# First queries in two parts, one more tile turned by TensorE, and other steps for batch 1

## The chip, the cores and the metric

The kernel runs on one core of one Trainium2 chip. A core has five engines that run side by side, each through its own list of instructions in order: TensorE (PE; its weight loads are shown apart as PEld), VectorE (DVE), ScalarE (ACT), GpSimd (POOL) and SyncE (SP). They wait for each other by semaphores. SP, ACT and POOL also issue DMA transfers, each in a queue of its own; sixteen DMA engines serve all queues. The metric is the device time of one execution in microseconds (us); eight runs of the kernel before have a median of 226.18 us.

## The reference

```python
# attention: q, k, v are (4, 8, 768, 64); mem_k, mem_v are (4, 8, 8, 64)
for c in range(24):                      # chunks of 32 queries
    keys   = concat(mem_k, k[c*32-16 : c*32+40])    # cut at both ends of the sequence
    values = concat(mem_v, v[same rows])
    a = softmax(q[c*32 : c*32+32] @ keys.T / 8)
    x[c*32 : c*32+32] = a @ values
# then a feed-forward block on x, now (4, 768, 512)
xn = (x - mean(x)) / sqrt(var(x) + 1e-6) * g_ln
out = x + max(xn @ w_ch1, 0) @ w_ch2     # w_ch1 (512, 2048), w_ch2 (2048, 512)
```

## The kernel before

The work is cut into 24 tiles of 128 rows, six for each of the four batches. Three tiles make a unit, so there are eight units (0 to 7). For each tile attention runs first: `scores` multiplies keys and queries of two groups of 64 rows on PE, `soften` takes the exponential on ACT, `values` multiplies by the values on PE, and DVE divides by the sums, takes the mean and scales (`norm` writes `xn`). `turn_x` then transposes `xn` into `xT`, which the feed-forward part reads: `up` and `up_tile` multiply by w_ch1 (a relu on DVE or ACT takes the result out of PSUM), `down` multiplies by w_ch2, and `finish` adds and writes the output through SP.

Keys and queries come in blocks of 256 rows, three to a batch. A block is loaded with four rows of eight heads on a partition (`load_block`, through POOL, in 16-bit), put in another order (`mix`), transposed, and copied in windows to `KT` (`window`, `pieces`, `key_right`, `key_left`) and to `QR`. Each group of keys has 8 columns of mem keys at its end (`memT`, `mem_cols`), and each group of values 8 rows of mem values (`v_mem`). The first block of batch 0 is loaded in 32 bit through SP and ACT and cast by `mix_raw` instead, so that it is there early.

Where `turn_x` transposes is set by `XU = 2`: tiles of the first two units (0 to 5) are turned by four PE matmuls against the identity and a DVE copy out of PSUM, all later tiles by a DMA transpose issued on SP.

The order of the instructions on every engine is that of the program text; no scheduler moves anything. Three parts matter here. The start (L445 to L594) is written out by hand: it loads, sets constants, and interleaves the first three tiles' attention with pieces of unit 0's `up_tile`. `warm` issues matmuls of zeros. From there on, a table `plan` holds what is to be issued beside the feed-forward work: unit u has 28 steps, of which 0 to 15 are `up` groups and 16 to 27 `down` groups (four of 4 matmuls for each of three tiles), and `at(u, step, ...)` puts a call behind that step's group. `attend(i, s0, s1, u)` places the scores, values, `norm` and `turn_x` of tile i. PSUM has two slots `att` for attention and transposes and four slots `mm` for feed-forward groups and key transposes; each is taken in turn, so that a group waits until the copy or relu that empties its slot is done.

Names and lines for the steps: loads of keys, queries and mem keys at the start L446 to L453; the cast of mem keys (`memk16` from `memkf`) L529; the first tile's chain L527 to L557; scores of the second tile L558; mem values' rows `v_mem` L133; `turn_x` L343; `pace_x` L361, a small POOL copy that reads `xT` of a tile so that the loads queued behind it on POOL start no earlier; batch 1's steps in units 0 and 1 L655 to L677.

Of the kernel before, what the change touches and what calls it, by code (L numbers as in the profile page):

```python
# [15 lines left out]
def kernel(  # L16
# [12 lines left out]
    nc = tc.nc  # L29
# [9 lines left out]
    HD = 65  # L39
    XU = 2  # L40
    NEG = -30000.0
# [209 lines left out]

    def mix_raw(which, srcs, half, eng):

        o = pick(iv, ("b", 0, 0, which))
        for par in range(2):
            copy(eng, free(o, 512 * half + 64 * par, [[128, 4], [1, 64]]),
                 free(srcs[par], 256 * half, [[64, 4], [1, 64]]))

# [84 lines left out]
    def turn_x(b, t):  # L343
        i = NT * b + t
        dst = xT[(i // 3) % 2][:, :, 128 * (i % 3) : 128 * (i % 3) + 128]
        if i // 3 >= XU:
            nc.sync.dma_start_transpose(out=dst, in_=xn[i % 4])
            return
# [97 lines left out]
    nc.scalar.dma_start(out=grow, in_=dram(moe_g_ln, 0, [[512, 1], [1, 512]]))  # L446
    for which in range(2):
        for par, eng in ((0, nc.sync), (1, nc.scalar)):
            eng.dma_start(
                out=raws[which][par],  # L450
                in_=dram((k, q)[which], 4 * par * HS, [[512, 32], [HS, 4], [1, 512]]),
            )
    nc.scalar.dma_start(out=memkf, in_=dram(mem_k, 0, [[64, 128], [128 * 64, 2], [1, 64]]))  # L453

# [4 lines left out]

    load_mem_v(0, nc.sync)  # L460

    PAIR = 1.0 / 128 + 15.0 / 2**20
# [19 lines left out]
    make_identity(nc, identity)  # L482
    nc.gpsimd.memset(V[0][0:32, 0, :, :], 0.0)
    ones(0, 0, NG, pool)
    nc.vector.memset(zero, 0.0)
# [7 lines left out]
    nc.vector.tensor_tensor(out=band[:, 1:2], in0=band[:, 1:2], in1=cnt[:, 2:3], op=ALU.add)  # L493
    nc.vector.tensor_scalar(out=band, in0=band, scalar1=NEG, scalar2=None, op0=ALU.mult)

    load_block(0, 1, 0)
    load_v(0, 0)
# [35 lines left out]
    mem_keys()  # L533
    mix_raw(1, raws[1], 0, dve)
    mix_raw(1, raws[1], 1, act)
    transpose_block(0, 0, 1, Q0)
    window(0, 0, K0, 0, dve)
    memT()
    window(0, 0, K0, 1, act)
    mem_cols(0, dve)  # L540
    whole_q(0, 0, Q0)
    warm(1, 512, p[:, 1, :])
# [3 lines left out]
    soften(0, 0, 1)  # L546
    window(0, 0, K0, 2, dve)
    window(0, 0, K0, 3, act)
    total(cnt[:, 0:1], 16, 128)
    count_v(0, 0, 0)  # L550
    mix(0, 1, 0, dve)
    transpose_block(0, 1, 0, Q0)
    v_mem(0, 0, 2, dve)
    window(0, 1, Q0, 0, dve)
    key_right(0, 3, dve)
    values(0, 0)
    norm(0, 0)  # L557
    scores(0, 1)  # L558
    soften(0, 1, 0)
    soften(0, 1, 1)  # L560
    window(0, 1, Q0, 1, act)
    v_mem(0, 2, 4, dve)
# [37 lines left out]
    def attend(i, s0, s1, u):  # L600

        b, t = divmod(i, NT)
        at(u, s0, scores, b, t)
        at(u, s0, soften, b, t, 0)
        at(u, s0 + 1, soften, b, t, 1)
        at(u, s1, values, b, t)
        at(u, s1 + 1, norm, b, t)
        at(u, s1 + (3 if i // 3 < XU else 2), turn_x, b, t)
        at(u, s1 + 2, stats, b, t)
        if i < 6:  # L610
            at(1, i % 3, root, b, t)
        else:
            at(i // 3 - 1, (20, 22, 23)[i % 3], root, b, t)
# [43 lines left out]
    at(0, 22, mix, 1, 0, 0, dve)  # L657
    at(0, 27, mix, 1, 0, 1, dve)
    at(0, 27, v_mem, 1, 0, 4, dve)
    at(1, 0, turn_keys, 1, 0)  # L660
    at(1, 1, more_keys, 1, 0)
    at(1, 1, turn_queries, 1, 0)
    at(1, 2, mix, 1, 1, 0, dve)
    at(1, 4, mix, 1, 1, 1, dve)
    attend(6, 4, 8, 1)
    at(1, 6, turn_keys, 1, 1)
    at(1, 7, more_keys, 1, 1)
    at(1, 10, turn_queries, 1, 1)
# [87 lines left out]
```

## Time and profile before

| | |
|---|---|
| median of 8 runs | 226.18 us (225.65 to 230.3) |
| the profiled execution's own time | 226.02 us |
| its span, first to last instruction | 224.2 us |
| PE busy | 211.3 us (94%), 1941 matmuls |
| PE weight loads | 130.5 us (58%) |
| DVE busy | 133.1 us (59%) |
| ACT busy | 103.2 us (46%) |
| POOL busy | 100.2 us (45%) |
| DMA | 27.85 MB in 72737 packets, mean 124 GB/s |

Busy time is a share of the span; on PE it is the engine in work, not at its peak. The profile's pages give lines of kernel.py as L and a number; a copy or matmul made by a helper has the helper's line (L104 is every copy on DVE, L102 on ACT, L218 every transpose of a key or query block, L378 the up groups, L389 the up groups of single tiles, L404 the down groups). A chain of waits is followed back from the last instruction: each row is what the next one waited for. The granted clock is what the throttle allows of TensorE's clock.

### The profile page before, as it was taken

To read this page: it belongs to the slowest core of one execution; us is meant where nothing else is said; L and a number is where in the kernel's file an instruction comes from. 1 tells how busy PE (TensorE), PEld (TensorE's weight loads), DVE (VectorE), ACT (ScalarE), POOL (GpSimd) and SP (SyncE) were. 2 spreads that over 40 slices of the span, in tenths; PEclk is the share of its full clock that TensorE was granted. 3 is DMA by queue.
4 is the path that set the end of the run, shared out by engine and by line. 5 is a ranking of instruction groups with operands and counts; after the bars stand their busy time and mean duration, and the time that the engine had idled before them with its cause. 6 is when DMAs were issued, how large, how long until landed. Compare 5 with 4: busy or idle time off the path is not lost.

```text
span 224.2 us, 4942 instructions
## 1 busy us (share of the span) xinstructions
PE 211.3 (94%) x1941; PEld 130.5 (58%) x1941; DVE 133.1 (59%) x330; ACT 103.2 (46%) x215; POOL 100.2 (45%) x172
## 2 busy tenths in 40 slices
PE   7569999997999889999999999999999999999994
PEld 2357986555664457545664566446654566456553
DVE  4585586687869638745585668725845367234221
ACT  4452558535783146641692067524761365103200
POOL 8936744899898479320933793400021011100000
PEclk9999999999999999999999999999999999999998
DMA  5999999699999999978897699485112203211012
GB/s 183 182 193 195 198 193 206 109 84 233 177 80 148 188 169 141 161 157 197 109 178 86 100 160 150 90 196 131 21 30 70 96 5 45 70 49 45 3 47 94
DMA packets 72737, 27.85 MB, mean 124 GB/s; under 512 B 60785, under 2 KB 68721, under 8 KB 72714
## 3 DMA queue, kind: packets, MB, share of 16 engines
q0 software_dynamic: 45728, 14.61, 63.6%
q1 hardware_dynamic: 26424, 12.34, 24.5%
q10 hardware_dynamic: 562, 0.59, 0.9%
q8 instruction: 15, 0.25, 0.5%
q14 instruction: 8, 0.07, 0.1%
HBM read 30.28 MB, written 6.29 MB: 163 GB/s over the span
## 4 chain that ended last, share of the span: by engine, by line
PE 80%; DVE 7%; DMA 6%; ACT 3%; issue 1%; ACTq 1%; DVEq 0%; SPq 0%
PE mm L378 33%; PE mm L404 30%; PE att L283 5%; DMA xT<-xn 4%; PE mm L389 4%; PE att L304 4%; DMA memkf<-in_mem_k_dram 2%; PE mm L218 2%; PE mm L426 2%; DVE xs L312 1%; ACT AT L293 1%; DVE KT L104 1%; DVE xn L324 1%; DVE V L104 1%; DVE iv L104 1%
## 5 line engine op out<-in xcount | busy, mean ns | idle before, releaser
L404 PE MATMUL mm<-w2c,rT 128*128 128x512 f16 x368 | 82.8, 379 | 0.0
L378 PE MATMUL mm<-xT,w1c 128*128 128x384 f16 x448 | 78.6, 327 | 2.8 <-DMA xT<-xn 1.6
L378 PEld LDWEIGHTS <-w1c 128*128 128x128 f16 x448 | 49.0, 114 | 25.2 <-DVE osb L413 2.1
L404 PEld LDWEIGHTS <-rT 128*128 128x128 f16 x368 | 34.9, 98 | 39.7
L370 ACT ACTIVATE rT<-mm 128x384 f16<-128x384 f32 (+1 forms) x63 | 31.4, 503 | 41.2 <-PE mm L378 23.1
L372 DVE TENSOR_SCALAR rT<-mm 128x384 f16<-128x384 f32 (+1 forms) x61 | 34.3, 568 | 26.3 <-PE mm L378 23.0
L293 ACT ACTIVATE AT<-att,band 104x512 f16<-104x512 f32 x48 | 31.3, 685 | 30.5 <-PE att L283 30.5
L128 POOL DMA_DIRECT2D V<-in_v_dram x48 | 38.3, 804 | 5.0 <-DMA w1c<-in_moe_w_ch_dram 3.4
L413 DVE SCALAR_TENSOR_TENSOR osb<-mm,rstd,xs 128x512 f32<-128x512 f32 x23 | 17.3, 751 | 34.0 <-PE mm L404 25.0
L335 POOL TENSOR_SCALAR veps<-sq 128x1 f32<-128x1 f32 x24 | 7.7, 319 | 59.8 <-ACT junk L329 46.1
L329 ACT ACTIVATE junk<-xs,nmean 128x512 f16<-128x512 f32 x24 | 17.4, 723 | 14.9 <-DVE nmean L318 13.6
L324 DVE SCALAR_TENSOR_TENSOR xn<-xs,nmean,gb 128x512 f16<-128x512 f32 x24 | 17.9, 748 | 0.5
L312 DVE SCALAR_TENSOR_TENSOR xs<-att,rec 128x512 f32<-128x512 f32 x24 | 16.6, 691 | 0.8
L283 PE MATMUL att<-QR,KT 64*104 64x64 f16 x384 | 16.1, 235 | 0.3 <-ACT QR L102 0.2
L339 POOL TENSOR_TENSOR rstd<-veps,mhalf 128x1 f32<-128x1 f32 x24 | 15.2, 634 | 2.0
L283 PEld LDWEIGHTS <-KT 64*104 64x104 f16 x384 | 12.8, 134 | 4.2 <-issue 2.8
L120 POOL DMA_DIRECT2D st<-in_q_dram x22 | 12.6, 588 | 3.7 <-DMA w2c<-in_moe_w_ch_dram 1.7
L389 PE MATMUL mm<-xT,w1c 128*128 128x128 f16 x192 | 13.8, 235 | 0.5 <-DVE xT L357 0.5
L120 POOL DMA_DIRECT2D st<-in_k_dram x22 | 13.1, 613 | 2.3 <-DMA w1c<-in_moe_w_ch_dram 1.8
L389 PEld LDWEIGHTS <-w1c 128*128 128x128 f16 x192 | 12.7, 119 | 1.1 <-issue 1.0
L304 PEld LDWEIGHTS <-AT 104*64 104x64 f16 x384 | 8.4, 114 | 7.5 <-issue 4.6
L311 DVE RECIPROCAL rec<-att 128x8 f32<-128x8 f32 x24 | 4.9, 205 | 12.7 <-PE att L304 12.5
(73 smaller groups left out, 142.6 us busy)
## 6 DMA issues: line engine op xcount, KB each, us to landing
out_dram<-osb SPq DMA_DIRECT2D x23, 256.0 KB, 2.3
V<-in_v_dram POOLq DMA_DIRECT2D x40, 96.0 KB, 5.6
st<-in_k_dram POOLq DMA_DIRECT2D x22, 128.0 KB, 5.6
st<-in_q_dram POOLq DMA_DIRECT2D x22, 128.0 KB, 6.3
w1c<-in_moe_w_ch_dram POOLq DMA_DIRECT2D x4, 512.0 KB, 9.6
w2c<-in_moe_w_ch_dram POOLq DMA_DIRECT2D x4, 512.0 KB, 8.7
V<-in_v_dram POOLq DMA_DIRECT2D x8, 80.0 KB, 4.8
xT<-xn SPq DMA_TRANSPOSE x18, 2.4
```

What stands on the lines that cost most here:

```text
L120: nc.gpsimd.dma_start(out=s[:, 512 * par : 512 * par + 512], in_=dram((k, q)[which], (b * H + 4 * par) * HS + blk * 256 * D, [[512, 32], [ ...
L128: nc.gpsimd.dma_start(out=V[b % 2][lo:hi, g, :, 0:64], in_=dram(v, b * H * HS + (64 * g - 16 + lo) * D, [[64, hi - lo], [HS, H], [1, 64]]),)
L283: nc.tensor.matmul(out=p[0:W, par, (4 * gg + j) * 64 : (4 * gg + j) * 64 + 64], lhsT=KT[b % 2][rows, 2 * t + gg, j, :], rhs=free(QR[b % 2] ...
L293: nc.scalar.activation(out=free(AT[t % 3], 32 * c, [[64, 16], [1, 32]]), in_=free(p, 4 * c, [[64, 16], [1, 4], [8, 8]], W), func=ACTF.Exp, ...
L312: nc.vector.scalar_tensor_tensor(out=x.rearrange("p (h d) -> p h d", h=8), in0=free(p, 0, [[128, 8], [1, 64]]), scalar=1.0, in1=free(r, 0, ...
L324: nc.vector.scalar_tensor_tensor(out=xn[i % 4], in0=xs[i % 9], scalar=nmean[t], in1=gb, op0=ALU.add, op1=ALU.mult,)
L329: nc.scalar.activation(out=junk, in_=xs[(NT * b + t) % 9], func=ACTF.Square, bias=nmean[t], scale=1.0, accum_out=sq[t],)
L370: nc.scalar.activation(out=o, in_=p, func=ACTF.Relu)
L372: nc.vector.tensor_scalar(out=o, in0=p, scalar1=0.0, scalar2=None, op0=ALU.max)
L378: nc.tensor.matmul(out=p, lhsT=free(w1c[c][:, dt, :], i, [[4, 128]]), rhs=xT[u % 2][:, dt, 128 * lo : 128 * (lo + n)], start=(dt == 0), st ...
L389: nc.tensor.matmul(out=p[:, 128 * k_ : 128 * k_ + 128], lhsT=free(w1c[c][:, dt, :], k_, [[4, 128]]), rhs=xT[u % 2][:, dt, 128 * i : 128 * ...
L404: nc.tensor.matmul(out=p, lhsT=rT[c][:, k_, 128 * i : 128 * i + 128], rhs=w2c[c][:, k_, :], start=(c == 0 and k_ == 0), stop=(c == 3 and k ...
```

## The change

- Queries of the first block are loaded as rows 0 to 63 and rows 64 to 127 of the partitions, each half on SP and ACT; mem keys move from ACT's fifth place to SP's second.
- POOL's load of block 1's keys moves ahead of the memsets of `V[0]`; most of the memset of the ones columns moves from POOL to DVE, which also takes `total` and `count_v` earlier.
- The first half of the queries is cast, transposed (`first_q`, eight matmuls of 64 columns) and copied (`first_copy`) before the first tile's scores; the second half follows after them. Block 1's key transposes move behind the first tile's values, and their window 0, window 2 of block 0 and `key_right` move from DVE to ACT (window 1 is ACT's in both). Four warm matmuls are added.
- `ON_PE` takes the place of `XU`: tile 8, unit 2's last, is turned by PE at step 19 of unit 1 instead of by DMA at step 18.
- Batch 1: the second `mix` moves from step 27 to 25 of unit 0, `v_mem` from step 27 of unit 0 to step 3 of unit 1, the mixes of block 1 from steps 2 and 4 to 5 and 6, its key transposes and windows from 6 and 7 to 7 and 8.

```diff
--- before.py
+++ after.py
@@ -37,7 +37,7 @@
     GW = 4 * W
     VW = 80
     HD = 65
-    XU = 2
+    ON_PE = (0, 1, 2, 3, 4, 5, 8)
     NEG = -30000.0
 
     ctx.enter_context(tc.manual_schedule())
@@ -249,12 +249,32 @@
         copy(eng, free(QR[b % 2], 1024 * blk + 64 * half, [[128, 8], [1, 64]]),
              free(pv, 64 * half, [[128, 8], [1, 64]]))
 
-    def mix_raw(which, srcs, half, eng):
-
-        o = pick(iv, ("b", 0, 0, which))
+    def mix_raw(which, srcs, half, eng, lo=0, hi=128):
+
+        o = pick(iv, ("b", 0, 0, which))[lo:hi, :]
+        r0, n = (0, 8) if half is None else (4 * half, 4)
         for par in range(2):
-            copy(eng, free(o, 512 * half + 64 * par, [[128, 4], [1, 64]]),
-                 free(srcs[par], 256 * half, [[64, 4], [1, 64]]))
+            copy(eng, free(o, 128 * r0 + 64 * par, [[128, n], [1, 64]]),
+                 free(srcs[par][lo:hi, :], 64 * r0, [[64, n], [1, 64]]))
+
+    def first_q(half, pvs):
+
+        i = pick(iv, ("b", 0, 0, 1))
+        rows = slice(64 * half, 64 * half + 64)
+        for r in range(8):
+            pv, c = (pvs[r // 4], 128 * (r % 4)) if len(pvs) == 2 else (pvs[0], 128 * r)
+            nc.tensor.matmul(
+                out=pv[:, c + 64 * half : c + 64 * half + 64],
+                lhsT=i[rows, 128 * r : 128 * r + 128], rhs=identity[rows, rows],
+                is_transpose=True, start=True, stop=True, tile_position=(64 * half, 0),
+            )
+
+    def first_copy(half, pvs):
+
+        n = 8 // len(pvs)
+        for m, pv in enumerate(pvs):
+            copy((dve, act)[m], free(QR[0], 512 * m + 64 * half, [[128, n], [1, 64]]),
+                 free(pv, 64 * half, [[128, n], [1, 64]]))
 
     def mix(b, blk, which, eng):
         s, o = pick(st, ("b", b, blk, which)), pick(iv, ("b", b, blk, which))
@@ -343,7 +363,7 @@
     def turn_x(b, t):
         i = NT * b + t
         dst = xT[(i // 3) % 2][:, :, 128 * (i % 3) : 128 * (i % 3) + 128]
-        if i // 3 >= XU:
+        if i not in ON_PE:
             nc.sync.dma_start_transpose(out=dst, in_=xn[i % 4])
             return
         p = slot("att")
@@ -444,13 +464,18 @@
 
     raws = ((osb[0], osb[1]), (osb[2], xs[4]))
     nc.scalar.dma_start(out=grow, in_=dram(moe_g_ln, 0, [[512, 1], [1, 512]]))
-    for which in range(2):
-        for par, eng in ((0, nc.sync), (1, nc.scalar)):
-            eng.dma_start(
-                out=raws[which][par],
-                in_=dram((k, q)[which], 4 * par * HS, [[512, 32], [HS, 4], [1, 512]]),
-            )
-    nc.scalar.dma_start(out=memkf, in_=dram(mem_k, 0, [[64, 128], [128 * 64, 2], [1, 64]]))
+
+    def first_load(which, par, lo, hi, eng):
+        eng.dma_start(
+            out=raws[which][par][4 * lo : 4 * hi, :],
+            in_=dram((k, q)[which], 4 * par * HS + 512 * lo, [[512, hi - lo], [HS, 4], [1, 512]]),
+        )
+
+    first_load(0, 0, 0, 32, nc.sync)
+    first_load(0, 1, 0, 32, nc.scalar)
+    nc.sync.dma_start(out=memkf, in_=dram(mem_k, 0, [[64, 128], [128 * 64, 2], [1, 64]]))
+    first_load(1, 0, 0, 16, nc.sync)
+    first_load(1, 1, 0, 16, nc.scalar)
 
     def load_mem_v(b, eng):
         eng.dma_start(
@@ -458,6 +483,8 @@
         )
 
     load_mem_v(0, nc.sync)
+    first_load(1, 0, 16, 32, nc.sync)
+    first_load(1, 1, 16, 32, nc.scalar)
 
     PAIR = 1.0 / 128 + 15.0 / 2**20
 
@@ -480,8 +507,9 @@
         copy(act, memv16[96:W, b, :, 0:64], xs[5 + b][96:W, :].rearrange("p (h d) -> p h d", h=8))
 
     make_identity(nc, identity)
-    nc.gpsimd.memset(V[0][0:32, 0, :, :], 0.0)
-    ones(0, 0, NG, pool)
+    load_block(0, 1, 0)
+    nc.gpsimd.memset(V[0].bitcast(FP32)[0:32, 0, :, :], 0.0)
+    ones(0, 0, 2, pool)
     nc.vector.memset(zero, 0.0)
     nc.vector.memset(gone, 1.0)
     clear_keys(0, dve)
@@ -492,8 +520,10 @@
     total(cnt[:, 2:3], 88, 96)
     nc.vector.tensor_tensor(out=band[:, 1:2], in0=band[:, 1:2], in1=cnt[:, 2:3], op=ALU.add)
     nc.vector.tensor_scalar(out=band, in0=band, scalar1=NEG, scalar2=None, op0=ALU.mult)
-
-    load_block(0, 1, 0)
+    ones(0, 2, NG, dve)
+    total(cnt[:, 0:1], 16, 128)
+    count_v(0, 0, 0)
+
     load_v(0, 0)
     load_v(0, 1)
     load_w1(0)
@@ -531,34 +561,39 @@
     warm(1, 128)
     transpose_block(0, 0, 0, K0)
     mem_keys()
-    mix_raw(1, raws[1], 0, dve)
-    mix_raw(1, raws[1], 1, act)
-    transpose_block(0, 0, 1, Q0)
+    warm(1, 512, mm[2])
     window(0, 0, K0, 0, dve)
+    mix_raw(1, raws[1], 0, dve, 0, 64)
+    mix_raw(1, raws[1], 1, act, 0, 64)
+    first_q(0, Q0)
     memT()
     window(0, 0, K0, 1, act)
     mem_cols(0, dve)
-    whole_q(0, 0, Q0)
+    first_copy(0, Q0)
     warm(1, 512, p[:, 1, :])
     scores(0, 0)
     mem_vals(0)
     soften(0, 0, 0)
     soften(0, 0, 1)
-    window(0, 0, K0, 2, dve)
-    window(0, 0, K0, 3, act)
-    total(cnt[:, 0:1], 16, 128)
-    count_v(0, 0, 0)
+    mix_raw(1, raws[1], None, dve, 64, 128)
+    rest = [as16(att[0][:, 0, :])]
+    first_q(1, rest)
+    v_mem(0, 0, 2, dve)
+    first_copy(1, rest)
+    warm(1, 512, mm[2])
     mix(0, 1, 0, dve)
-    transpose_block(0, 1, 0, Q0)
-    v_mem(0, 0, 2, dve)
-    window(0, 1, Q0, 0, dve)
-    key_right(0, 3, dve)
     values(0, 0)
     norm(0, 0)
+    window(0, 0, K0, 2, act)
+    window(0, 0, K0, 3, act)
+    transpose_block(0, 1, 0, Q0)
+    window(0, 1, Q0, 0, act)
+    window(0, 1, Q0, 1, act)
+    key_right(0, 3, act)
+    warm(2, 512, p[:, 1, :])
     scores(0, 1)
     soften(0, 1, 0)
     soften(0, 1, 1)
-    window(0, 1, Q0, 1, act)
     v_mem(0, 2, 4, dve)
     turn_x(0, 0)
     turn["mm"] = 3
@@ -605,7 +640,7 @@
         at(u, s0 + 1, soften, b, t, 1)
         at(u, s1, values, b, t)
         at(u, s1 + 1, norm, b, t)
-        at(u, s1 + (3 if i // 3 < XU else 2), turn_x, b, t)
+        at(u, s1 + (3 if i in ON_PE else 2), turn_x, b, t)
         at(u, s1 + 2, stats, b, t)
         if i < 6:
             at(1, i % 3, root, b, t)
@@ -655,16 +690,16 @@
     at(0, 20, count_v, 1, 0, 0)
     at(0, 20, count_v, 1, 1, NG - 1)
     at(0, 22, mix, 1, 0, 0, dve)
-    at(0, 27, mix, 1, 0, 1, dve)
-    at(0, 27, v_mem, 1, 0, 4, dve)
+    at(0, 25, mix, 1, 0, 1, dve)
+    at(1, 3, v_mem, 1, 0, 4, dve)
     at(1, 0, turn_keys, 1, 0)
     at(1, 1, more_keys, 1, 0)
     at(1, 1, turn_queries, 1, 0)
-    at(1, 2, mix, 1, 1, 0, dve)
-    at(1, 4, mix, 1, 1, 1, dve)
+    at(1, 5, mix, 1, 1, 0, dve)
+    at(1, 6, mix, 1, 1, 1, dve)
     attend(6, 4, 8, 1)
-    at(1, 6, turn_keys, 1, 1)
-    at(1, 7, more_keys, 1, 1)
+    at(1, 7, turn_keys, 1, 1)
+    at(1, 8, more_keys, 1, 1)
     at(1, 10, turn_queries, 1, 1)
     at(1, 11, v_mem, 1, 4, 8, dve)
     attend(7, 11, 14, 1)
```

## The prediction

> **What bounds the kernel now.** I read the page first (PE busy 94% of a 224.2 us span), then the gaps of PE by stretches, then the chain of waits, then the timeline around each gap. By stretches (columns: stretch, its length, then busy us of PE, PEld, DVE, ACT, POOL, clock, DMA share, GB/s):
>
> ```profile
> 5.00:10.60 5.60, 3.03 (x25) 2.09 (x25) 2.57 (x11) 2.69 (x8) 5.55 (x9) 1.00 1.39 190
> 10.60:16.67 6.07, 4.03 (x61) 3.27 (x60) 5.22 (x16) 3.89 (x9) 2.66 (x4) 1.00 1.48 192
> 49.50:53.50 4.00, 2.91 (x28) 2.07 (x27) 3.93 (x9) 1.49 (x6) 4.00 (x6) 1.00 1.27 214
> 53.50:67.50 14.00, 13.95 (x169) 9.24 (x169) 9.79 (x27) 11.18 (x26) 12.40 (x23) 1.00 1.42 151
> 67.50:80.00 12.50, 10.89 (x64) 5.35 (x62) 8.93 (x20) 2.84 (x9) 7.44 (x15) 1.00 1.22 190
> 80.00:127.80 47.80, 47.80 (x415) 28.04 (x414) 30.39 (x70) 23.76 (x46) 25.16 (x42) 1.00 1.18 139
> ```
>
> From 80 us on PE has no gap, and from 17 to 49.5 us almost none, so time is to be won in three places only: the start, 49.5 to 53.5, and just before 80. The chain of waits (start, us, what) names what holds PE there:
>
> ```profile
> 2.61 5.32 DMA memkf<-in_mem_k_dram
> 7.95 0.23 DVE memk L104
> 8.18 0.66 DVE iv L104 x2
> 8.89 1.05 PE mm L218 x8
> ...
> 50.66 1.26 DVE V L104
> 51.95 0.56 DVE rT L372
> ...
> 70.63 8.72 DMA xT<-xn
> 79.35 0.14 issue
> ```
>
> At the start DVE stands at the cast of mem keys, which land at 7.93 although the queries landed at 6.28 and 7.35. At 50.66 a copy of mem values stands ahead of a relu. At 70.63 tile 8's transpose takes 8.72 us to land behind a burst of loads. The timeline prices the last two at PE (in brackets: idle before, releaser) and shows the clock:
>
> ```profile
> 16.67 1.86 PE L389 MATMUL mm<-xT,w1c 128*128 128x128 f16 x16 [0.52 <-DVE xT L357]
> 22.69 1.06 PE L389 MATMUL mm<-xT,w1c 128*128 128x128 f16 x16
> 52.56 0.81 PE L378 MATMUL mm<-xT,w1c 128*128 128x384 f16 x4 [0.96 <-DVE rT L372]
> 69.81 0.75 DVE L324 SCALAR_TENSOR_TENSOR xn<-xs,nmean,gb 128x512 f16<-128x512 f32 x1
> 69.92 0.61 PE L218 MATMUL mm<-identity,iv 128*128 128x128 f16 x8
> 79.49 0.81 PE L378 MATMUL mm<-xT,w1c 128*128 128x384 f16 x4 [1.61 <-DMA xT<-xn]
> ```
>
> The same 16 matmuls take 1.86 us at 16.67 and 1.06 at 22.69, though the granted clock reads 1.00 throughout: PE runs at about half rate until some 21.5 us.
>
> **Part 1a: first scores sooner.** Before, scores start at 10.59. After, SP carries keys, mem keys, then the first 64 rows of queries; ACT keys, then its 64 rows. Bytes ahead of these rows' landing: keys 0.52 MB + mem keys 0.07 + half the queries 0.26 = 0.85 MB. SP's and ACT's queues moved 288 GB/s from 2.0 to 5.4 us; POOL's packets appear only at 5.4, 2.8 us after POOL's first issue (2.61). That issue now comes ahead of two memsets, at about 1.3, so POOL's packets join at about 4.1. By 4.1 0.60 MB are moved; 0.25 MB remain at two thirds of 188 to 288 GB/s: 1.3 to 2.0 us, to 5.4 or 6.1. The slowest share lands later still (SP's queries were moved by about 5.0, landed at 6.28): 0.8 to 1.3 us. So 6.2 to 7.4; I take 6.9. Mem keys, ahead on the same queue, come before that and hold nobody.
>
> [...]
>
> From landing to scores: DVE two casts of 0.29, two memT copies 0.44, mem columns 0.26, half a query copy 0.25, hand-overs 0.15: 1.7 (ACT: 0.80 + 0.51 + 0.37, the same). Scores at 8.6: 2.0 earlier.
>
> **Part 1b: the order behind them.** In before, from scores (10.59) to the first tile's first values of tile 1 (18.53) are 7.94 us. After, counted from the scores: two casts of 64x512 at 0.55 (estimate: twice the 0.29 of 256 elements) to 1.15; eight transposes of 64 columns, not in the trace, between 0.42 (the four mem-key ones) and 1.05 (eight full ones), taken as 0.85, to 2.0; query copy 0.42 to 2.45, which values wait for since they write the same bank; the softmax (ends at 2.2) is no longer last. Values 0.65 to 3.15. Only now come the eight transposes of block 1 (before: ahead of values): 1.05 to 4.2; then ACT, not DVE, copies windows, 0.46 + 0.51 + 0.20, to 5.4, while two warm matmuls (0.43 each) hide under ACT. Scores of tile 1 0.90 to 6.3; only behind them tile 0's turn (xn is ready at 5.0): 0.62, copy 0.44 to 7.4; up 1.86 to 9.3. That is 1.4 later than 7.94. So part 1 nets 2.0 - 1.4 = **+0.6**, with ends -1.0 (queries land at 7.9, casts and transposes at their high ends) and +1.2 (landing 6.2).
>
> Later loads don't eat this: w1's second quarter lands at 16.47 and is first used at 19.45; w2's last at 40.45, used after 45; POOL's stream is limited by bytes, which haven't changed. The memset and counts that DVE takes over (0.7 + 0.26 + 0.23) end near 4.0, under the wait for the second half of keys (4.64).
>
> **The clock.** [...] Four warm matmuls now fill gaps, between transposes and waits. If the switch comes before the first up group, that shrinks 1.86 to 1.06, with scores (0.90 to 0.65) and transposes (1.05 to 0.61): up to +1.5 more. [...]
>
> **Part 2: unit 1's start.** V's mem rows (1.26) and the second mix (0.45) leave the chain at 50. Mix now stands before the second finish, so the third ends 0.3 to 0.45 late and its PSUM slot releases the second up group as late. PE's gaps 0.96 + 0.18 go: 1.14 - 0.3 = **+0.85** (0.4 to 1.1). Mem rows at step 3 and mixes at 5 and 6 meet DVE between relus, four slots deep; DVE was busy 9.79 of 14.0 us there. Moving the mixes also passes waits of 0.34 and 1.32 for their loads. Cover gone, one relu late by about 1 us.
>
> **Part 3: tile 8 by TensorE.** Removed: 1.61 idle at 79.49. Tile 7's transpose landed at 73.5, so nothing else holds xT. Added: four transposes, 0.39 (the row at 47.29), and a wait: at step 19 PE arrives at 69.92 to 70.07 while xn ends at 70.56: 0.5 to 0.65. Queued behind it are unit 1's last key transposes and eight groups of down, hence the whole core. The DVE copy (0.41) hides in down. SP loses one transpose; POOL's pace copy is released some 4 us earlier (it waited 3.68), so batch 2's V loads start then; nobody needs them before unit 3. **+0.6** (0 to 1.3).
>
> **Sum.** The profiled execution took 226.02, its span 224.2 and 1.8 around it; the median is 0.16 above. Gains 0.6 + 0.85 + 0.6 = 2.05: the span becomes 222.1, the median 226.18 - 2.05 = **224.1**.
>
> **Rivals.**
> - Clock early (0.18): the extra +1.5, about half of it kept: 223.0 to 222.4. [...]
> - Start gives nothing (0.22): the queries land no sooner than 7.35 to 7.9, since POOL's loads now share the engines from 4.1, while the 1.4 of part 1b is paid: start -1.0, total +0.45, 225.7. For: rates fell to 188 GB/s when POOL's packets joined. Decided where scores start: at 10 or later.
> - Slower (0.12): the clock switches late. [...]
> - The forecast (0.48): 223.1 to 225.0 as its own range.
>
> Within 0.5% (1.13 us) a measurement of this kernel can't be told from no change. The forecast and the early clock lie below 225.05 but for a little: faster 0.64; same 0.24; slower 0.12. Range: 222.3, with the early clock in, to 226.6, with the empty start; what is left out is most of the late clock and a little below.
>
> **What would show it.** Right: scores at 8 to 9 us; no gap over 0.3 at 50 to 53; no gap before unit 2, but one of about 0.5 ahead of tile 8's transposes near 68; first up group at about 16. Wrong: memkf landing after 7; scores after 10; 16 matmuls at 1.9 us after 23; relus waiting for mem rows at step 3; or new gaps in PE after 80 where faster PE meets late loads.

## The result, and the profile after

The changed kernel has a median of 225.52 us (20 runs, 224.32 to 226.4). The kernel before has 227.12 us (57 runs, 225.54 to 230.74; the eight known at the time of the prediction had 226.18). The ratio is 0.993, with a 95% interval of 0.9911 to 0.995: **faster by 0.7%, or 1.6 us**, where 2.05 were forecast. (All ratios leave out runs over 1.5% above the fastest of their kernel, the medians leave out none, so the two need not agree.) The gain came out near the forecast. Its parts did not.

The two profiled executions must be read with care. That of after took 226.43 us (span 224.6), 0.9 above its median; that of before 226.02 (span 224.2), 1.1 below its median. Side by side they show after 0.4 *slower*. They say where the time lies inside each execution; how much a part is worth must come from the medians.

By stretches, the profile after (columns: stretch, its length, busy us of PE, PEld, DVE, ACT, POOL, clock, DMA share, GB/s):

```profile
5.00:10.57 5.57, 3.30 (x24) 1.72 (x23) 2.65 (x11) 2.40 (x8) 4.03 (x6) 1.00 1.22 191
10.57:17.20 6.63, 5.72 (x72) 3.99 (x72) 4.98 (x12) 4.63 (x14) 3.62 (x5) 1.00 1.47 197
49.50:53.50 4.00, 3.96 (x35) 2.85 (x34) 3.39 (x9) 2.09 (x7) 4.00 (x7) 1.00 1.36 150
53.50:67.50 14.00, 12.62 (x147) 8.21 (x146) 9.20 (x24) 9.44 (x22) 10.99 (x20) 1.00 1.50 171
67.50:80.60 13.10, 12.44 (x88) 6.14 (x85) 10.07 (x25) 4.04 (x11) 11.26 (x21) 1.00 1.17 174
```

The idle stretch at 49.5 to 53.5 is gone (PE busy 3.96 of 4.00, before 2.91). A new one stands right behind it: 53.5 to 67.5 had 13.95 busy and now has 12.62. From 80.6 on PE has no gap in either kernel. The timeline of PE after names the places (in brackets: idle before, releaser):

```profile
9.49 0.61 PE L266 MATMUL mm<-identity,iv 64*128 64x64 f16 x8 [1.65 <-DVE iv L104]
...
10.57 0.90 PE L303 MATMUL att<-QR,KT 64*104 64x64 f16 x16
...
17.20 1.87 PE L409 MATMUL mm<-xT,w1c 128*128 128x128 f16 x16 [0.52 <-DVE xT L377]
...
19.98 1.91 PE L409 MATMUL mm<-xT,w1c 128*128 128x128 f16 x16
...
57.72 0.62 PE L218 MATMUL mm<-identity,iv 128*128 128x128 f16 x8 [0.77 <-DVE iv L104]
...
60.58 0.81 PE L398 MATMUL mm<-xT,w1c 128*128 128x384 f16 x4 [0.43 <-DVE rec L331]
...
71.90 0.40 PE L372 MATMUL att<-identity,xn 128*128 128x128 f16 x4 [0.66 <-DVE xn L344]
```

Scores start at 10.57, as before (10.59), with PE waiting 1.65 for the first queries. The gaps at 57.72 and 60.58 are new. The one at 71.90 is tile 8's turn, and the 1.61 before unit 2 is gone. DVE's timeline tells what the new gaps wait for:

```profile
57.24 0.43 DVE L104 COPY iv<-st 128x1024 f16<-128x1024 f16 x1 [2.24 <-DMA st<-in_k_dram]
...
58.95 0.59 DVE L104 COPY iv<-st 128x1024 f16<-128x1024 f16 x1 [0.81 <-DMA st<-in_q_dram]
```

These are the two mixes of batch 1's block 1, at steps 5 and 6. DVE stands 2.24 us at the first, because its loads have not landed; relus and the division of tile 6 queue behind it. The chain of waits (start, us, what) says where that lateness begins. In before it ran over DVE and PE from 8 us on; now, up to 59 us, it is POOL's stream of loads:

```profile
3.35 7.32 DMA V<-in_v_dram
10.68 0.28 issue
10.96 9.86 DMA w1c<-in_moe_w_ch_dram
...
21.11 9.79 DMA w2c<-in_moe_w_ch_dram
...
31.18 8.05 DMA w2c<-in_moe_w_ch_dram
...
46.35 0.75 POOL V L128
47.10 2.35 POOL V L128 x3
49.45 1.59 POOL st L120 x3
51.03 7.82 DMA st<-in_q_dram
58.95 0.52 DVE iv L104
```

Each large load is issued 0.28 after an earlier one has landed (10.96, 21.11, 31.18), and the loads for batch 1 come behind them on the same engine. Up to 59 us nothing in this chain waits for PE.

### The profile page after: what moved, and what is told of

Its sections match the earlier page's. It is cut to its first block, busy times and chain, and to the rows that moved or that the text cites. A ratio compares the mean times of both kernels' runs of the same rounds, so it can differ in the third digit from the quotient of the medians.

```text
span 224.6 us, 4976 instructions
## 1 busy us (share of the span) xinstructions
PE 213.7 (95%) x1957; PEld 130.9 (58%) x1957; DVE 133.0 (59%) x330; ACT 103.9 (46%) x220; POOL 98.8 (44%) x172
## 4 chain that ended last, share of the span: by engine, by line
PE 69%; DMA 19%; POOL 6%; DVE 3%; issue 1%; DVEq 0%; POOLq 0%
PE mm L398 30%; PE mm L424 30%; DMA w2c<-in_moe_w_ch_dram 8%; DMA w1c<-in_moe_w_ch_dram 4%; PE att L303 4%; DMA st<-in_q_dram 3%; DMA V<-in_v_dram 3%; PE att L324 3%; PE mm L446 2%; POOL V L128 1%; POOL st L120 1%; POOL rstd L359 1%; DVE xs L332 1%; DVE KT L104 0%; DVE iv L104 0%
## 5 line engine op out<-in xcount | busy, mean ns | idle before, releaser
L355 POOL TENSOR_SCALAR veps<-sq 128x1 f32<-128x1 f32 x24 | 6.9, 286 | 61.4 <-ACT junk L349 47.7
L359 POOL TENSOR_TENSOR rstd<-veps,mhalf 128x1 f32<-128x1 f32 x24 | 15.7, 656 | 2.0
```

Of the source, the lines that this page charges most:

```text
L359: nc.gpsimd.tensor_tensor(out=rstd[(NT * b + t) % 9], in0=veps[t % 3], in1=mhalf, op=ALU.pow)
```

## The experiments

Parts 1, 2 and 3 are those of the prediction: the start, batch 1's steps, tile 8 on PE. Every ratio is to the kernel before, run in the same session on the same chip; its own runs in the three sessions are the last rows.

The mean granted clock of every run is on record, not only that of the traced one. It is either 0.997 or more, or 0.993 or less; no run lies between. A mean of 0.992 over 226 us is what 3.6 us would give at a clock of 0.50, the lowest that a stretch of pool_loads shows (its row 48.00:50.00 below). The last column counts the runs at 0.993 or less, and gives the median of the others.

| kernel | what it is | median us (range, runs) | ratio, 95% interval | at 0.993 or less; median of the others |
|---|---|---|---|---|
| after | parts 1, 2, 3 | 225.52 (224.32 to 226.4, 20) | 0.9930, 0.9911 to 0.9950 | 0 of 20; 225.52 |
| only1 | part 1 | 226.17 (225.28 to 228.97, 22) | 0.9968, 0.9941 to 0.9994 | 2 of 22; 226.13 |
| only2 | part 2 | 226.90 (224.95 to 230.05, 22) | 0.9985, 0.9957 to 1.0013 | 8 of 22; 226.44 |
| only3 | part 3 | 226.23 (225.14 to 227.26, 22) | 0.9939, 0.9916 to 0.9962 | 0 of 22; 226.23 |
| no1 | parts 2, 3 | 225.78 (224.76 to 226.27, 11) | 0.9934, 0.9903 to 0.9964 | 0 of 11; 225.78 |
| late_burst | before, batch 2's loads later | 225.73 (224.22 to 232.4, 22) | 0.9935, 0.9905 to 0.9964 | 2 of 22; 225.64 |
| pool_late | after, POOL's start as before | 225.71 (223.64 to 228.01, 15) | 0.9937, 0.9905 to 0.9969 | 1 of 15; 225.44 |
| memk_sp | no1, mem keys second on SP | 225.76 (224.65 to 227.98, 22) | 0.9937, 0.9912 to 0.9961 | 1 of 22; 225.75 |
| later | no1, two steps later | 224.76 (223.82 to 226.72, 10) | 0.9906, 0.9868 to 0.9944 | 0 of 10; 224.76 |
| no1_loads | no1, block 1 loaded earlier | 226.31 (225.23 to 229.2, 22) | 0.9972, 0.9944 to 1.0001 | 6 of 22; 225.91 |
| after_loads | after, block 1 loaded earlier | 226.25 (225.22 to 227.51, 22) | 0.9964, 0.9941 to 0.9988 | 7 of 22; 226.09 |
| pool_loads | pool_late, block 1 loaded earlier | 228.17 (226.0 to 229.3, 22) | 1.0056, 1.0032 to 1.0079 | 21 of 22; 226.00 |
| best | pool_loads, tile 8 turned a step later | 227.48 (224.92 to 228.8, 22) | 1.0010, 0.9983 to 1.0038 | 19 of 22; 225.09 |
| before | beside only1, only2, only3, no1 | 227.28 (225.34 to 230.9, 64) | 1 | 15 of 64; 226.79 |
| before | beside late_burst, pool_late, memk_sp, later | 227.23 (225.48 to 230.14, 56) | 1 | 15 of 56; 226.85 |
| before | beside the last four kernels | 227.12 (225.52 to 231.49, 75) | 1 | 21 of 75; 226.59 |

The next table is read off PE's and POOL's timelines of the profiled executions: where each piece starts, in us. "Unit 1 part" is from unit 1's first up group to the values of tile 8, and "turn part" from there to unit 2's first up group. Within a part, what the start of that one execution happened to be drops out.

| kernel | scores | first up group | POOL's first values load for batch 1 | unit 1 starts | values of tile 8 | unit 2 starts | unit 1 part | turn part |
|---|---|---|---|---|---|---|---|---|
| before | 10.59 | 16.67 | 45.12 | 49.24 | 66.94 | 79.49 | 17.70 | 12.55 |
| only1 | 10.36 | 16.98 | 46.08 | 49.55 | 68.31 | 80.23 | 18.76 | 11.92 |
| only2 | 10.68 | 16.92 | 45.37 | 49.49 | 67.24 | 80.17 | 17.75 | 12.93 |
| only3 | 10.50 | 16.57 | 45.03 | 49.15 | 66.83 | 78.55 | 17.68 | 11.72 |
| no1 | 10.00 | 16.25 | 45.34 | 48.82 | 66.33 | 78.15 | 17.51 | 11.82 |
| after | 10.57 | 17.20 | 46.29 | 49.76 | 68.11 | 79.94 | 18.35 | 11.83 |
| pool_late | 9.19 | 16.45 | 46.29 | 48.10 | 67.48 | 79.32 | 19.38 | 11.84 |
| later | 11.04 | 17.11 | 46.21 | 49.68 | 67.17 | 78.17 | 17.49 | 11.00 |
| late_burst | 10.58 | 16.65 | 45.11 | 49.22 | 66.92 | 77.69 | 17.70 | 10.77 |

### The parts alone

Part 1 alone is after with these lines set back (and with them the lines of `turn_x` that read `ON_PE`, and block 1's key transposes and windows to steps 6 and 7):

```diff
-    ON_PE = (0, 1, 2, 3, 4, 5, 8)
+    XU = 2
...
-    at(0, 25, mix, 1, 0, 1, dve)
-    at(1, 3, v_mem, 1, 0, 4, dve)
+    at(0, 27, mix, 1, 0, 1, dve)
+    at(0, 27, v_mem, 1, 0, 4, dve)
...
-    at(1, 5, mix, 1, 1, 0, dve)
-    at(1, 6, mix, 1, 1, 1, dve)
+    at(1, 2, mix, 1, 1, 0, dve)
+    at(1, 4, mix, 1, 1, 1, dve)
```

> Only part 1 (the start: split queries, mem keys sooner, POOL's early load, the new order) on the kernel before. By the forecast it gains 0.6 us. By the profile after, where the queries' first rows landed at 8.46 and 8.92 and the first up group started at 17.20 against 16.67, it loses about 0.5 us. If instead the profiled execution was an unlucky one, the first up group starts at 16 to 16.7 here.

Measured: 0.9968 (0.9941 to 0.9994), 0.7 us faster by the ratio, near the 0.6 of the forecast, where the trace of after had made me expect a loss. In its own trace scores start at 10.36 and the first up group at 16.98, 0.31 later than before, and unit 1's part takes 18.76 us, 1.06 more than before. So the one traced execution shows no place where part 1 gains, and the median says that it does; what the gain is stays open.

Part 2 alone is before with the steps of the change:

```diff
-    at(0, 27, mix, 1, 0, 1, dve)
-    at(0, 27, v_mem, 1, 0, 4, dve)
+    at(0, 25, mix, 1, 0, 1, dve)
+    at(1, 3, v_mem, 1, 0, 4, dve)
...
-    at(1, 2, mix, 1, 1, 0, dve)
-    at(1, 4, mix, 1, 1, 1, dve)
+    at(1, 5, mix, 1, 1, 0, dve)
+    at(1, 6, mix, 1, 1, 1, dve)
...
```

> Only part 2 (other steps for batch 1). By the forecast it gains 0.85 us: no gap of PE at 50 to 53. By the profile after, the gap only moves to the key transposes of block 1, which wait for a mix that waits for its loads (DVE idle 2.24 us there): then it gains 0 to 0.3 us. If those loads are late only because part 1 delayed POOL by 1.2 us, the wait is missing here and the gain is 0.85.

Measured: 0.9985 (0.9957 to 1.0013), no change that can be told. The gaps of 0.96 and 0.18 near 52 are gone; gaps of 0.86 and 0.18 stand at 59 to 61 instead, and unit 1's part takes 17.75 against 17.70. In this profile the DMA transpose of tile 8 landed later still, so PE waited 1.99 at 80.17, where before waited 1.61.

Part 3 alone:

```diff
-    XU = 2
+    ON_PE = (0, 1, 2, 3, 4, 5, 8)
...
-        if i // 3 >= XU:
+        if i not in ON_PE:
...
-            at(u, s1 + (3 if i // 3 < XU else 2), turn_x, b, t)
+            at(u, s1 + (3 if i in ON_PE else 2), turn_x, b, t)
```

> Only part 3 (tile 8 turned by PE). By the forecast it gains 0.6 us (1.61 idle gone, 1.0 of wait and transposes added). A rival: the landing of tile 8's transpose behind a burst of loads (8.72 us in the profiled execution) varies from run to run and makes the scatter of the kernel before (225.5 to 230.7 us against 224.3 to 226.4 after); then this part alone gains 1.5 to 2 us in the median and its runs lie within about 2 us of each other.

Measured: 0.9939 (0.9916 to 0.9962), 1.4 us by the ratio; nearly the whole effect of the change in one part. In its profile the turn part falls by 0.83. Its runs also lie within 2.1 us of each other, where those of before beside it span 5.6. The last column of the table tells why: 15 of those 64 runs of before are at a clock of 0.993 or less (median 228.95), and none of only3's 22. Among the others the medians are 226.79 and 226.23, 0.56 apart.

Parts 2 and 3, that is all but part 1, are both diffs on before.

> Parts 2 and 3 without part 1. By the forecast 1.45 us faster than before (0.6 less than the whole change). If part 1 costs 0.5 us, this is 2.1 us faster than before and beats the whole change.

Measured: 0.9934 (0.9903 to 0.9964), 225.78, 1.5 us by ratio and medians, as the forecast had it for these two parts (1.45). After is 225.52: on top of them part 1 adds 0.26 to the medians, well inside both intervals. Against part 3 alone part 2 gives 0.45, inside the intervals too. What the runs establish is part 3. Part 1 alone is clear of no change, though its addition to the others is not; part 2 alone cannot be told from no change.

### Why tile 8's transpose was late

Before, with the loads of batch 2's blocks put behind the pace copy, which reads tile 8's `xT`, so that they start only when its transpose has landed (the pace copy itself stands one step sooner):

```diff
-            at(w - 1, 0 if b == 3 else 21, load_pair, b, blk)
+            at(w - 1, 0 if b == 3 else 24, load_pair, b, blk)
...
-        at(w - 1, 24, pace_x, 6 * b - 4)
+        at(w - 1, 24 if b == 3 else 23, pace_x, 6 * b - 4)
```

> The kernel before, tile 8 still turned by DMA, but batch 2's twelve block loads stand on POOL behind the pace copy that waits for tile 8's turn, instead of ahead of it. If the burst of loads makes tile 8's transpose late and its lateness makes the scatter, the transpose lands in about 3 us instead of 8.7, PE's gap before unit 2 is gone, the runs lie as close as those with part 3 alone, and the median gains 1.4 to 1.9 us (no transposes on PE and no wait for xn, unlike part 3). If a DMA transpose is slow there for another reason, gap and scatter stay.

Measured: 0.9935 (0.9905 to 0.9964), as much as part 3 gives, with tile 8 still turned by DMA. The group of the three DMA transposes issued from 61 to 71 us shows why. First the kernel before:

```profile
L347 SPq DMA_TRANSPOSE xT<-xn x3: 1189/1192/1302, 61.3 to 70.6; - x3
...
DMA to landing us min/median/max: 3.8/6.0/8.7
```

and then the same group with the later loads:

```profile
L347 SPq DMA_TRANSPOSE xT<-xn x3: 1189/1192/1332, 61.2 to 70.6; - x3
...
DMA to landing us min/median/max: 2.4/2.5/4.8
```

Issued at the same times, they land within 2.4 to 4.8 us instead of 3.8 to 8.7 (tile 8 last: 2.4 against 8.7), and PE's gap before unit 2 is gone (the turn part falls from 12.55 to 10.77). The lateness came from the burst of loads, as the prediction had it. Its cure by order costs PE no wait and no transposes, and so its profile is the shortest of all (span 222.4). But its runs scatter widely still, from 224.2 to 228.1 with one at 232.4. Falls of the clock are rarer than in before (2 of 22 runs, one of them that at 232.4, against 15 of 56), but the other 20 runs still span 3.9 us. So the late transpose is not the only thing that varies between runs; what else does stays open, since only one execution of each kernel was traced.

### Why the first scores did not come sooner

After, with POOL's start in the old order:

```diff
-    load_block(0, 1, 0)
-    nc.gpsimd.memset(V[0].bitcast(FP32)[0:32, 0, :, :], 0.0)
-    ones(0, 0, 2, pool)
+    nc.gpsimd.memset(V[0][0:32, 0, :, :], 0.0)
+    ones(0, 0, NG, pool)
+    load_block(0, 1, 0)
...
-    ones(0, 2, NG, dve)
```

> The changed kernel with POOL's part of the start as before (memsets whole on POOL, then the load of block 1's keys; no memset on DVE). If POOL's early load is what makes keys and queries land late (5.53, 8.46, 8.92), the second half of the keys lands at 4.6 to 4.9 and the first rows of queries by 7.0, the scores start at 8.7 to 9.0 and the first up group at about 15.6; 1 to 1.5 us faster than the changed kernel at that place. If instead mem keys ahead on SP or the split make them late, queries land after 8.2 as in the changed kernel and nothing is gained.

The issues of the first 12 us (transfer, queue, number, KB each, median us to landing), before:

```profile
osb<-in_q_dram SPq DMA_DIRECT2D x1, 256.0 KB, 4.8
xs<-in_q_dram ACTq DMA_DIRECT2D x1, 256.0 KB, 5.4
...
memkf<-in_mem_k_dram ACTq DMA_DIRECT2D x1, 64.0 KB, 5.3
```

after:

```profile
xs<-in_q_dram ACTq DMA_DIRECT2D x2, 128.0 KB, 6.8
osb<-in_q_dram SPq DMA_DIRECT2D x2, 128.0 KB, 6.8
...
memkf<-in_mem_k_dram SPq DMA_DIRECT2D x1, 64.0 KB, 4.8
```

and after with POOL's old start:

```profile
xs<-in_q_dram ACTq DMA_DIRECT2D x2, 128.0 KB, 5.8
osb<-in_q_dram SPq DMA_DIRECT2D x2, 128.0 KB, 5.1
...
memkf<-in_mem_k_dram SPq DMA_DIRECT2D x1, 64.0 KB, 3.7
```

For SP's halves only the first one's landing is on record. With half as many bytes it took 6.8 us in after, where the whole had taken 4.8 in before; with POOL's load put back it takes 5.1, and mem keys 3.7 instead of 4.8. In absolute times the first halves land at 8.46 and 8.92 in after and at 7.00 and 7.20 here, and scores start at 9.19. The three kernels with part 1 and POOL's old start (pool_late, pool_loads, best) have scores at 9.19, 8.99 and 8.56; the three with part 1 and POOL's load first (after, only1, after_loads) at 10.57, 10.36 and 10.31. (The memset that goes back from DVE to POOL with it is not on the path: DVE casts the first keys at 3.81 in after and at 3.93 here.) So the early load on POOL, made in the same part, took away what the split of the queries gave.

What the three queues moved from 4 to 6 us shows how (packets, MB, share; q1 and q10 are SP's and ACT's, q0 is POOL's). Before:

```profile
q10 hardware_dynamic: 296, 0.29, 47.0%
q1 hardware_dynamic: 183, 0.24, 33.3%
```

after:

```profile
q0 software_dynamic: 160, 0.15, 46.9%
q10 hardware_dynamic: 45, 0.08, 22.8%
q1 hardware_dynamic: 253, 0.08, 19.6%
```

SP and ACT together moved 0.53 MB in these two microseconds before, 0.16 after and 0.35 with POOL's old start, while POOL moved 0.03, 0.15 and 0.05. In after POOL's packets begin between 3.9 and 4.0, as the prediction had it (4.1); but what was left to SP and ACT then is 0.16 MB in 2 us, 80 GB/s, where it had counted on 125 to 192.

Yet the median with POOL's old start is 225.71, against 225.52 for after: the earlier start of the scores brings nothing. PE's timeline for this kernel shows where it went:

```profile
9.19 0.90 PE L303 MATMUL att<-QR,KT 64*104 64x64 f16 x16
10.98 0.61 PE L266 MATMUL att<-identity,iv 64*128 64x64 f16 x8 [0.89 <-DVE iv L104]
...
16.45 1.05 PE L409 MATMUL mm<-xT,w1c 128*128 128x128 f16 x16 [0.52 <-DVE xT L377]
...
57.26 0.62 PE L218 MATMUL mm<-identity,iv 128*128 128x128 f16 x8 [1.86 <-DVE iv L104]
```

The second halves land at 9.12 on ACT and, by the cast on DVE that waits for it until 10.16, near 10.1 on SP, later than they are wanted: 0.89 is given back at once. What is left (the first up group is 0.75 ahead), with the full clock that this execution already has at 16.45, makes unit 1 start 1.66 us ahead of after (48.10 against 49.76), and there the mix of block 1 waits for its load as long as ever: the gap is 1.86 where after has 0.77. POOL's first values load for batch 1 was issued at 46.29 in both. PE gets there sooner and waits longer. The matmuls at 16.45 run at full rate here already (1.05 for 16), which the page's clock row does not announce, as it reads 1.00 in after too, where they take 1.87; that gain too ends in this wait.

Mem keys second on SP instead of fourth on ACT, alone, on no1:

```diff
+        if which == 0:
+            nc.sync.dma_start(out=memkf, in_=dram(mem_k, 0, [[64, 128], [128 * 64, 2], [1, 64]]))
...
-    nc.scalar.dma_start(out=memkf, in_=dram(mem_k, 0, [[64, 128], [128 * 64, 2], [1, 64]]))
```

> Parts 2 and 3 with the start of the kernel before, except that mem keys go second on SP, ahead of the whole queries. If mem keys' small packets ahead of the queries delay them, SP's queries land after 8 and scores start at 10.5 or later. If not, mem keys land by 6.3, queries at 6.5 to 7.5, scores start near 10.0 and the median is 0 to 0.5 us below that of parts 2 and 3 alone (225.8).

Measured: 0.9937 (0.9912 to 0.9961), the same as no1. The first of the two expectations came true: mem keys land at 4.95 (7.58 in no1), but SP's queries at 8.14 instead of 5.98 and ACT's at 7.97 instead of 6.71, and scores start at 10.57. The stream of SP and ACT ends near 8 either way (7.58 with mem keys in no1, 8.14 with SP's queries here); the order only chose which of its members was last. This run is also the one to hold against pool_late for the split: both have mem keys second on SP and POOL's old start. Whole, the queries land at 7.97 and 8.14; in halves, the first halves at 7.00 and 7.20 and the second at 9.12 and near 10.1. The first halves come about 1 us sooner, and the second 1 to 2 us later.

### Why part 2's gain went again

On no1, the mix of block 1's queries moves three steps on, and tile 8's turn one:

```diff
-        at(u, s1 + (3 if i in ON_PE else 2), turn_x, b, t)
+        at(u, s1 + (4 if i == 8 else 3 if i in ON_PE else 2), turn_x, b, t)
...
-    at(1, 6, mix, 1, 1, 1, dve)
+    at(1, 9, mix, 1, 1, 1, dve)
```

> Parts 2 and 3 without part 1, and two steps later: the mix of block 1's queries at step 9 of unit 1 instead of 6, and tile 8's turn at step 20 instead of 19. If the gaps that parts 2 and 3 leave (0.55 and 0.18 near 58 to 60, 0.65 near 70) come from that mix waiting for its load and from xn being 0.6 late at step 19, they are gone and the kernel is 1.0 to 1.4 us faster than parts 2 and 3 alone: about 224.6. If loads for key blocks hold PE there in another way, less than 0.3.

Measured: 224.76 (ratio 0.9906, 0.9868 to 0.9944), 1.0 below no1 and the fastest of all the kernels run. Its interval overlaps those of no1 and of after (0.9911 to 0.995), so it beats before for certain and these two only in the median. PE's timeline:

```profile
60.62 0.62 PE L218 MATMUL att<-identity,iv 128*128 128x128 f16 x8 [0.86 <-DVE iv L104]
...
71.46 0.39 PE L352 MATMUL att<-identity,xn 128*128 128x128 f16 x4
```

Tile 8's turn no longer waits (0.65 in no1), and the turn part falls from 11.82 to 11.00. In unit 1 one gap remains where no1 had two. This execution had POOL's loads as late as after's (46.21); with the mix at step 9 that did not matter (17.49 against 18.35).

The other cure is to load block 1 sooner. On no1, on after, and on the kernel with POOL's old start, POOL issues it directly behind the mem values:

```diff
-    order += [(load_pair, (1,)), (mem_cols, (pool,)), (load_v, (4,)), (load_v, (5,))]
+    order += [(mem_cols, (pool,)), (load_v, (4,)), (load_v, (5,))]
...
-    order[1:1] = [(mem_v_loads, ()), (early, ())] + [(root0, (t,)) for t in range(3)]
+    order[1:1] = [(mem_v_loads, ()), (load_pair, (1,)), (early, ())] + [(root0, (t,)) for t in range(3)]
```

> Parts 2 and 3 without part 1, and on POOL the loads of batch 1's block 1 ahead of the memsets for batch 1 instead of behind them and the first four loads of values. If PE's gaps at 58 to 60 come from these loads landing at 54 to 57 us, they land by 47 here, the gaps are gone and the median is 0.5 to 0.8 us below 225.8. If DVE's work alone makes the gaps, nothing changes.

> The changed kernel with the same move of batch 1's block 1 loads. Its gaps after 56 us (0.77, 0.43, 0.17) go: about 1.0 to 1.3 us below its 225.5.

> The changed kernel with POOL's part of the start as before, and the same move of the loads. Theory: the load stream, which doesn't move with PE, took what the earlier start won (gap 1.86 at 55 against 0.77), so that this start was worth nothing (225.7 against 225.5). Then with the loads out of the way it is worth what it wins at the start, 0.7 to 1.2 us against the changed kernel with the same move, and near 223.5. If the earlier start is lost in another way, the two are equal.

The fourth adds the later turn of tile 8 to the third:

```diff
-            at(u, s1 + (3 if i in ON_PE else 2), turn_x, b, t)
+            at(u, s1 + (4 if i == 8 else 3 if i in ON_PE else 2), turn_x, b, t)
```

> The last one, and tile 8's turn at step 20 of unit 1 instead of 19, so that PE doesn't wait for xn (0.66 us near 70). 0.4 to 0.7 us below the last one, about 223.

All four expectations failed on the time: 226.31, 226.25, 228.17 and 227.48. They held on the cause: block 1 lands by 48, and PE's gaps from 54 to 61 are gone in all four, so it was the loads that DVE stood for there. But a new wait stands in front. The timelines of pool_loads, first POOL's:

```profile
41.80 1.26 POOL L120 DMA_DIRECT2D st<-in_k_dram  x2 [1.90 <-DMA w2c<-in_moe_w_ch_dram]
43.23 1.14 POOL L120 DMA_DIRECT2D st<-in_q_dram  x2 [0.16 <-issue]
44.40 0.74 POOL L493 MEMSET V<- 104x768 f32 x1
45.20 0.62 POOL L651 MEMSET V<- 32x640 f16 x1
```

then DVE's:

```profile
45.85 1.20 DVE L104 CAST V<-cnt 104x128 f16<-104x128 f32 x2 [2.97 <-POOL V L651]
46.68 0.74 DVE L344 SCALAR_TENSOR_TENSOR xn<-xs,nmean,gb 128x512 f16<-128x512 f32 x1
```

then PE's:

```profile
47.48 0.40 PE L372 MATMUL att<-identity,xn 128*128 128x128 f16 x4 [2.67 <-DVE xn L344]
```

On POOL the memsets of batch 1's `V` stand behind the four loads, which themselves wait for `w2c` to land. Here they run from 44.40. In after they ran from 40.11:

```profile
40.11 0.74 POOL L493 MEMSET V<- 104x768 f32 x1
```

On DVE, `count_v` writes into the same `V` and stands ahead of `xn` of a tile that PE is to turn. PE waits 2.67 us from 44.81 on, 1.16 from 45.78 in after_loads and 2.99 from 44.44 in best: the earlier PE was, the longer. In no1_loads, where these memsets run from 43.17, it waits 0.62. I had counted the loads' own wait and not what is queued behind them.

For the sum of pool_loads that is not all. By stretches (the last three columns: clock, DMA share, GB/s):

```profile
44.00:48.00 4.00, 1.33 (x9) 0.53 (x8) 2.11 (x5) 0.61 (x1) 3.62 (x9) 0.97 0.74 108
48.00:50.00 2.00, 2.00 (x6) 0.76 (x5) 1.77 (x6) 1.43 (x4) 1.67 (x5) 0.50 0.00 0
50.00:52.00 2.00, 2.00 (x11) 0.91 (x10) 0.64 (x1) 0.52 (x2) 2.00 (x3) 0.70 0.01 1
52.00:54.00 2.00, 2.00 (x15) 1.21 (x14) 2.00 (x5) 0.00 (x0) 2.00 (x5) 1.00 1.13 86
```

Behind the wait the granted clock falls to 0.50 and is back at 1.00 only by 52. The clock stood at 0.50 for about (4.00 x 0.03 + 2.00 x 0.50 + 2.00 x 0.30) / 0.50 = 3.4 us, which costs half of it, 1.7. The account: 2.67 + 1.7 new, 1.86 and the smaller 0.27 and 0.18 of pool_late removed, +2.1 in all; the medians differ by 228.17 - 225.71 = 2.46.

For no1_loads and after_loads, without a fall of the clock, the same account gives +0.15 (0.88 new, 0.73 removed) and +0.05 (1.42 new, 1.37 removed); their medians lie 0.5 and 0.7 higher. For no1_loads the table's last column has the rest: 6 of its 22 runs had a lower clock, none of no1's 11, and the others' median lies 0.13 above no1's. After_loads has 7 of 22 such runs, against none, and the others still lie 0.57 above after, which isn't explained. That the fall of the clock in pool_loads is no accident of the traced execution the same column shows: 21 of its 22 runs have it, and 19 of 22 in best. The three runs of best without it have a median of 225.09, so the fourth expectation's 223 was missed even there.

## Why the prediction was right, and where not

**The total.** Forecast 224.1, 2.05 below the median then known; measured 225.52, 1.60 below that of the larger set (1.1 to 2.0 by the interval). The eight runs known then were low by 0.9, so the time itself came 1.4 above the forecast, outside the 223.1 to 225.0 given as the forecast's own range and inside the wider one. The direction and about the size of the gain were right, but with luck: part 1a failed in its mechanism, part 2's gain went again, and what made up for them is that runs with a lower clock are rare with part 3, which the prediction did not weigh.

**Part 1a: wrong.** First scores were to start at 8.6, on landings at 6.2 to 7.4, taken as 6.9. They landed at 8.46 and 8.92, and scores started at 10.57: the gain was 0.02 instead of 2.0. The failing step is "0.25 MB remain at two thirds of 188 to 288 GB/s". That POOL's packets join at about 4.1 was right (3.9 to 4.0); but from 4 to 6 us SP and ACT then moved 80 GB/s instead of 125 to 192. At that rate 0.25 MB take 3.1 us, to 7.2, and with the 0.8 to 1.3 of the slowest share 8.0 to 8.5, near the 8.46 and 8.92 measured. The second keys too came 0.9 late (5.53 against 4.64), and pool_late shows that 1.4 to 1.7 us of the halves' landing are due to POOL's early load. A second step failed with it: "Mem keys, ahead on the same queue, come before that and hold nobody". In memk_sp they hold both queues' queries, by 2.16 and 1.26 us. What follows the landing was right: from 8.92 to the scores are 1.65 us (1.7 forecast). The rival "start gives nothing" described this, with its mark, scores at 10 or later, and its 225.7 lies nearer the measured median than the forecast does. Its 7.35 to 7.9 for the queries (the 7.9 stands under part 1's lower end too) were nearer than the 6.9 taken, but no run shows the 7.9: the first halves land at 8.46 and 8.92 in after and at 7.00 and 7.20 in pool_late. What the split itself gives, pool_late shows against memk_sp: the first halves land about 1 us sooner than the whole (7.97 and 8.14), and the scores, which need only them, start at 9.19 instead of 10.57.

**Part 1b: right in sign, too large.** From scores to the values of tile 1 were to be 9.3 us instead of 7.94; they are 8.43, against 7.87 for before in the same view (10.59 to 18.46), 0.56 more instead of 1.4. The estimates for what the trace didn't have were high: the 64x512 cast takes 0.42 (0.55 estimated), the eight 64-column transposes 0.61 (0.85).

**Part 1, the later loads: wrong.** "Later loads don't eat this ... POOL's stream is limited by bytes, which haven't changed." The three kernels traced with part 1 and block 1's loads in their old place have POOL's first values load for batch 1 at 46.08 to 46.29; of those without it, all but one at 45.03 to 45.37, and that one, `later`, at 46.21. So this looks like a cost of part 1 of up to 1 us, though one execution without it shows the same. It meets part 2's mixes: unit 1's part takes 18.35 in after against 17.51 in no1.

**Part 2: half right.** The 0.96 and 0.18 are gone, as forecast. The text had the danger in a clause ("moving the mixes also passes waits of 0.34 and 1.32 for their loads") and took those as gone. They move with PE only if the loads do; the loads keep POOL's time, and with part 1 POOL was later. Hence 2.24 and 0.81 of waiting on DVE, 0.77 + 0.43 + 0.17 on PE, and no net gain: +0.85 forecast, -0.05 (only2) and +0.19 (no1) in the profiles' unit 1 part, -0.65 in after's.

**Part 3: right in mechanism, and in size for a run at full clock.** Within the profiles every term came as worked out: a wait of 0.66 ahead of the turn (0.5 to 0.65 forecast), 0.40 of transposes (0.39), no gap before unit 2, and 0.72 from the turn part (12.55 to 11.83; 0.6 forecast). Among runs at 0.997 or more only3's median lies 0.56 below that of before. The ratio makes 1.4 us of it and the medians of all runs 1.05, since runs with a lower clock, 51 of before's 195 and 2.2 to 2.8 us longer in the median, are 2 of 100 in the six kernels with part 3 and block 1's loads in their old place (only3, no1, after, later, memk_sp, pool_late). The prediction put this at nothing: it was sized from one execution of before without such a fall. That a still later transpose of tile 8 brings the fall about is argued, not shown, since no run of before with a fall was traced: only2, with 9.00 us for tile 8 and a wait of 1.99 in its profile, has 8 in 22, and late_burst, without the wait, 2 in 22.

**The clock.** No shift at the start of after's traced execution: 16 matmuls take 1.87 and 1.91 at 17.20 and 19.98 and 1.06 from 23.22 on, as in before (1.86 at 16.67, 1.91 at 19.45, 1.06 at 22.69). Neither the early nor the late rival happened there. The early one's sum was off: 1.5 with half of it kept leads to 222.6 to 223.4, not to 222.4 to 223.0. For the late one (0.12, and most of what the range leaves out) no run shows a price: in each of the 14 traced executions the 16 matmuls take 1.06 to 1.08 by 23.22 at the latest. What the runs show in its place is a fall of the clock behind a wait, where 3.4 us at 0.50 cost 1.7 (pool_loads).

## What to carry to other kernels

A transfer that is put first can be paid for by those already under way (with POOL's load first, SP's first half took 6.8 us to land instead of 5.1): look at the landing of every transfer beside it, on all queues, and not only at its own. When a wait is moved in front of an instruction that needs a load, check what the load's own queue waits for; if that queue keeps its own time, PE's earlier arrival is only a longer wait (1.86 in pool_late, 0.77 in after), and where the load is moved forward in its queue, what is queued behind it comes later (the memsets in pool_loads run from 44.40, in after from 40.11). Size a part from the median of runs with it alone, since two profiled executions of these kernels could differ by as much as the whole effect, in the wrong direction (after's 0.4 above that of before, where the medians lie 1.6 apart the other way), and look at the granted clock of every run: an edit can be worth as much by how often the clock falls as by the wait that it removes (only3: 1.4 by the ratio, 0.56 among the runs at 0.997 or more).

## What the hardware showed that was not expected

- A PE idle of 2.67 us (pool_loads) was followed by 3.4 us at a granted clock of 0.50, one of 2.99 (best) by about 6.0 (from PE's return at 47.43 to 53.4); idles of 1.16 (after_loads), 1.86 (pool_late) and 1.99 (only2) in the traced executions were followed by no fall. Of the 22 runs of each, 21 of pool_loads and 19 of best show a lower mean clock. By these lengths the fall cost 1.7 us beyond the wait itself in pool_loads and about 3.0 in best.
- The switch to full rate at the start does not follow from the program alone. In pool_late the 16 matmuls at 16.45 already took 1.05; in pool_loads and best, whose start is the same text, they took 1.87 at 15.98 and 15.39. The granted clock read 1.00 in all three, so there the half rate is to be read from the matmuls' durations.
- Tile 8's DMA transpose of 128x512 landed in 2.4 us with batch 2's block loads put behind it (late_burst), and in 8.7 and 9.0 us behind a burst of them (before, only2).
- Loads issued sooner on POOL slowed those that SP and ACT already had under way: 0.16 MB in 2 us in after, 0.35 in pool_late.
